# Block 1 of a fused attention and gated-FFN kernel: six plain tiles and three pairs by seven products, and token lists for the head and blocks 0 and 1

## The chip, the cores and the metric

The kernel runs on one core of a Trainium2 chip. The core has a matrix engine (PE, whose weight loads the profile lists apart as PEld), a vector engine (DVE), a scalar engine (ACT), a general engine (POOL) and a queue that issues DMAs (SP). Each works through its own list of instructions in order, and they meet through semaphores. The metric is device time in microseconds (us) of one execution.

## The reference

The first half is an attention without a score matrix, for 8 batches, 8 heads, 576 tokens and 64 channels; the second is a feed-forward block with a gated GELU on 4608 rows of 512 channels.

```python
q_s = exp(q - max(q, -1)); q_s = q_s / (sum(q_s, -1) + 1e-9)      # over the 64 channels
k_s = exp(k - max(k, 2));  k_s = k_s / (sum(k_s, 2) + 1e-9)       # over the 576 tokens
kv  = einsum('bhsd,bhse->bhde', k_s, v)
x   = einsum('bhsd,bhde->bhse', q_s, kv)      # rearranged to (4608, 512)
g   = x @ w_gate                               # (4608, 1536)
out = (0.5 * g * (1 + erf(g / sqrt(2))) * (x @ w_val)) @ w_out
```

Inputs and output are 32-bit floats; the kernel multiplies in 16-bit floats and sums in 32.

## The kernel before, in words

**Blocks.** There are nine feed-forward blocks of 512 rows, in the order 0 to 6, 8, 7. Blocks 0 to 7 take 512 of the 576 tokens of one batch each; block 8 takes the 64 left over from each. Beside a block's feed-forward the engines prepare the attention of the next batch: ACT takes the exponentials of q and k, DVE sums and inverts the norms (`norm_sum`), POOL multiplies them in (`norm_mul`), v is cast to 16 bits, PE forms kv (`unit_kv`, `unit_kv4`) and then x (`unit_x`, `unit_x4`), and copies bring x from PSUM into `xt`.

**A plain tile.** The 1536 hidden channels are 12 tiles of 128. A plain tile takes four matmuls of 512 columns for the gate (g) and four for the value (v); ACT applies Gelu to the gate's bank, DVE multiplies both into `ht`. Blocks 0 and 1 work so.

**Seven products.** In blocks 2 to 8 two tiles three apart (k and k + 3, for k in 0, 1, 2, 6, 7, 8) are one pair: a two by two block product, formed by seven products in place of eight, as in Strassen's and Winograd's scheme (`product_gv`). Each product is four matmuls of 256 columns, 28 for a pair. The price is paid elsewhere: sums of weights (`sum_wgv` for pairs 0 to 2, `sum_w1` for the others, once in the kernel), four sums of x per block (`sum_x`), copies and snapshots of PSUM banks on ACT and DVE, and sums into a buffer `cc`. The sum of weights with number 3 is written over a weight block, so that from then on those tiles can't be taken as plain ones.

**The output.** Blocks 1 to 8 use seven products there too (`product`, 12 matmuls of 256 columns each), with sums of `ht` (`sum_h`) and differences of `w_out` (`sum_w`, the tensors `tw`); block 0 uses 48 plain matmuls of 512 columns.

**Order.** Nothing is reordered by a compiler: the program's order is each engine's order. Blocks 2 to 8 are written as token lists, `PROG[b]`, that `play` reads. Tokens that matter here, for a pair k: `kP1` to `kP7` are its products (PE, banks a, b, c of the pair); `kc` copies bank a to b (ACT); `ks2`, `ks5` are snapshots; `ka2`, `ka5` sums into `cc` (DVE); `kg2`, `kg4`, `ku` Gelu (ACT); `km2`, `km4` (DVE) and `kU` write `ht`. For plain tile t: `tg`, `tv`, `tga`, `tva`. For the block: `x0` to `x3` are sums of x; `NA`, `NB`, `M0` to `M3` the next batch's norms; `K`, `X` its kv and x products, `Xa`, `Xd` the copies of x; `O1` to `O7` products of the output; `s..` sums of `ht`; `y1`, `y2`, `y5` snapshots of output banks, `b+`, `c+`, `a+` the sums into the rows to be stored, `ye` the last copy; `TE`, `TG` load ACT's tables for Exp and Gelu. A last letter d, a or p names DVE, ACT or POOL. A sign `<` in front takes the token for the block before.

**The head and blocks 0 and 1** are not lists. The head is straight code after the loads: norm sums and products of q, matmuls that only keep PE busy (`warm_pe`), transposes (`t_mm`, `t_out`), sums of exp k (`ksum_mm`), casts of v in three parts on three engines (`cast_vn`), kv (`kv_mm`, `kv_norm`) and x. Block 0's feed-forward is `ffn_first` for two tiles and `ffn_group` for the rest; its output is the loop over `mm_out`, cut at tiles 6 and 11. Block 1 calls `ffn_first`, `ffn_fi`, then `out_strassen`. What rides beside them is hung on by `at(block, kind, index, ...)` and issued by `ride`. Among it are the POOL sums of `wg` and `wv` with number 3, hung on `(1, NS, 0)`, which is after the first matmuls of block 1's output.

**PSUM** has eight banks: six in a ring (`big`), two for attention (`small`), until `one_ring` joins them.

**Buffers of sums.** One of the two `cc` buffers is a view of an `eq` tile (`cc_b`), the other a tile of its own.

Of the kernel before, what the change touches and what calls it, by code (L numbers as in the profile page):

```python
# [9 lines left out]
f32 = mybir.dt.float32  # L10
# [8 lines left out]
def kernel(  # L19
# [16 lines left out]
    P = 128  # L36
# [85 lines left out]
    for i in range(2):  # L122
# [15 lines left out]
    cc_b = [x.rearrange("p j n c -> p (j n c)").bitcast(f32)[:, 0:1024].rearrange(  # L138
        "p (i t r) -> p i t r", i=2, t=2) for x in eq_b]

# [65 lines left out]
    def cast_w_o(c, eng="pool", i0=0, i1=2):  # L206
        copy_on(eng, wo_sb[:, 2 * c + i0:2 * c + i1, :], wst[("wo", c, i0)])
# [10 lines left out]
    def cast_vn(b, j, cuts, engs):  # L218
        for n0, n1, eng in zip(cuts, cuts[1:], engs):
            copy_on(eng, v16_b[0][:, n0:n1, 2 * j:2 * j + 2, 0:D].rearrange("p n a d -> p a n d"),  # L220
                    tiles[("v", b)][:, 2 * j:2 * j + 2, n0 * D:n1 * D].rearrange("p a (n d) -> p a n d", d=D))
# [72 lines left out]
    def kv_norm(b, j, engs=("dve", "act")):  # L294
        for hh, eng in enumerate(engs):
            o, i, r = (st[(b, "kv")][:, hh, j, :], st[(b, "pskv")][hh][:, j, 0:D],
                       st[(b, "rck")][hh][:, j:j + 1])
            if eng == "act":
                nc.scalar.activation(out=o, in_=i, func=ACTF.Copy, scale=r)
            else:  # L300
                nc.vector.tensor_scalar(out=o, in0=i, scalar1=r, scalar2=None, op0=ALU.mult)

    def unit_kv(b):
        for j in range(2):
# [6 lines left out]
        for j in range(2):  # L311
            kv_norm(b, j)
# [13 lines left out]
    def kv4_norm(b):  # L326
        kv = st[(b, "kv")] = kv_tile(b)
        for hh, ps in enumerate(st[(b, "pskv4")]):
# [4 lines left out]
            if id(ps) in held:  # L333
                let_go(ps)
# [7 lines left out]
    def t_mm(b, j):  # L342
        pst = st[(b, "pst", j)] = small([P, NT - 1, P], f16, "pst") if b else big([P, NT - 1, P], f16, "pst")
        for n in range(NT - 1):
            nc.tensor.transpose(pst[:, n], buf(eq_b, b)[:, j, n + 1], ident)

    def t_out(b, j, eng):
        copy_on(eng, get_eqt(b)[:, j], st[(b, "pst", j)].rearrange("p n (h m) -> p h n m", h=2))

# [38 lines left out]
    def unit_x(b, j, spare, engs=("act", "dve")):  # L388
        px = [bank([P, MAIN], "psx", spare) for _ in range(2)]
        x_mm(b, j, px, xq)  # L390
        st[(b, "x", j)] = px
        if engs:
            x_out(b, j, engs)

    def x_out(b, j, engs=("act", "dve")):
        for t, eng in enumerate(engs):
            xt_out(b, j, t, eng, st[(b, "x", j)][t])

    def xt_out(b, j, t, eng, ps):

        copy_on(eng, get_xt(b)[:, 2 * j + t, :].rearrange("p (c m u) -> p c u m", c=(NT - 1) // 2, u=2),
                ps.rearrange("p (u c m) -> p c u m", c=(NT - 1) // 2, u=2))
# [19 lines left out]
    def x4_out(b, t, eng):  # L422
# [678 lines left out]
```

## Time and profile before

| | us |
|---|---|
| median of three runs (290.77 to 291.0) | 290.77 |
| the profiled execution | 290.9 |
| its span | 288.9 |
| head, up to block 0's first gate matmul | 14.66 |
| block 0's output starts | 36.12 |
| block 1 starts | 49.43 |
| block 1's output starts | 70.26 |
| block 2 starts | 83.85 |
| first product 5 of block 3 | 112.20 |

The span runs from the first to the last recorded instruction; about 2 us of the execution lie around it. A time in the trace is counted from the span's start. In a line of the timeline the first two numbers are the start and the length of the (merged) piece, then come engine, source line, operation, tile written, tiles read, and the number of instructions; in square brackets stands the idle time before it and what ended it. PE's pieces end later than the next one starts, since matmuls are pipelined; the distance from start to start is what one costs. In a line of waits stand the total in us, the number of times and the longest.

### The profile page before, as it was taken

The page shows a single profiled execution, that of the slowest core. Times are in us where ns is not written, and L with a number is a line of the kernel's source. Part 1 is how long each engine was busy: PE and PEld are TensorE (multiplying, and loading weights), DVE is VectorE, ACT ScalarE, POOL GpSimd, SP SyncE. Part 2 cuts the span into 40 slices and gives each one's busy share as a digit, 9 for nine tenths or more (in the row PEclk, how much of TensorE's full clock was granted, in tenths as well). Part 3 has the DMA queues.
Part 4 walks back from the last instruction along what each step waited for, and adds up shares of the span by engine and source line. Part 5 has one row for each costly group of instructions (what it writes and reads, how often), then busy time and mean ns, then how long its engine had stood idle before and what let it go on. Part 6 is the DMA issues. An engine that isn't in the chain of part 4 may idle for free.

```text
span 288.9 us, 7376 instructions
## 1 busy us (share of the span) xinstructions
PE 279.0 (97%) x2923; PEld 215.7 (75%) x2923; DVE 244.6 (85%) x491; ACT 209.5 (73%) x379; POOL 137.3 (48%) x130
## 2 busy tenths in 40 slices
PE   8799999999699999999999999999999999999994
PEld 2444444445578887888888888888888888888884
DVE  2736785587989999889999999999999899998993
ACT  3763485885388888988998899889795477716840
POOL 1867557499539640855874337541643104110110
PEclk9999999999999999999999999999999999999999
DMA  7999999958119925339139953690305030003304
GB/s 272 385 383 388 409 407 407 390 208 197 44 75 350 272 47 190 122 53 303 57 99 237 377 175 147 181 241 0 147 1 84 2 146 2 0 2 74 75 0 147
DMA packets 39122, 51.26 MB, mean 177 GB/s; under 512 B 16304, under 2 KB 22704, under 8 KB 39088
## 3 DMA queue, kind: packets, MB, share of 16 engines
q1 hardware_dynamic: 38368, 49.36, 52.2%
q10 hardware_dynamic: 720, 1.44, 1.3%
q8 instruction: 23, 0.38, 0.5%
q14 instruction: 11, 0.09, 0.1%
HBM read 37.75 MB, written 9.44 MB: 163 GB/s over the span
## 4 chain that ended last, share of the span: by engine, by line
PE 67%; DVE 4%; ACT 1%; issue 1%; DVEq 0%
PE psa L594 25%; PE psc L594 12%; PE psA L673 11%; PE psb L594 6%; PE psC L673 6%; PE psB L673 3%; PE pskv L321 1%; PE psa L673 1%; DVE sh L550 1%; PE psx L386 1%; DVE ht L800 1%; PE psc L673 0%; DVE cc L766 0%; DVE xt L193 0%; ACT L441 0%
## 5 line engine op out<-in xcount | busy, mean ns | idle before, releaser
L594 PEld LDWEIGHTS <-wgv_sb 128*128 128x128 f16 x672 | 65.7, 98 | 8.0 <-issue 0.2
L239 POOL TENSOR_TENSOR eq<-eq,rrq 128x576 f16<-128x576 f16 (+1 forms) x28 | 34.5, 1244 | 25.1 <-ACT psb L782 10.8
L673 PEld LDWEIGHTS <-ht 128*128 128x128 f16 x384 | 37.2, 98 | 5.2 <-issue 0.4
L594 PE MATMUL psa<-xs,wgv_sb 128*128 128x256 f16 x288 | 40.4, 273 | 0.0
L446 PEld LDWEIGHTS <-wgv_sb 128*128 128x128 f16 x192 | 18.6, 98 | 23.0 <-issue 1.3
L782 ACT COPY psb<-psa 128x512 f32<-128x512 f32 x42 | 24.3, 585 | 9.2 <-PE psa L594 7.2
L231 DVE TENSOR_REDUCE rq<-eq 128x18 f32<-128x1152 f16 (+1 forms) x16 | 21.2, 1324 | 5.2 <-ACT eq L213 5.0
L763 ACT ACTIVATE snq<-psc 128x512 f32<-128x512 f32 x35 | 20.7, 605 | 5.7 <-PE psc L594 5.6
L446 PE MATMUL psg<-xt,wgv_sb 128*128 128x512 f16 x96 | 23.8, 379 | 0.5 <-DVE xt L193 0.4
L446 PE MATMUL psv<-xt,wgv_sb 128*128 128x512 f16 x96 | 23.8, 379 | 0.0
L673 PEld LDWEIGHTS <-sh 128*128 128x128 f16 x192 | 18.5, 98 | 5.3 <-DVE sh L550 2.1
L213 ACT ACTIVATE ek<-kt 128x1152 f16<-128x1152 f32 (+1 forms) x11 | 17.7, 1605 | 5.6 <-issue 4.4
L594 PE MATMUL psb<-xt,wgv_sb 128*128 128x256 f16 x144 | 21.6, 273 | 0.1
L594 PE MATMUL psa<-xt,wgv_sb 128*128 128x256 f16 x144 | 20.9, 273 | 0.0
L810 POOL TENSOR_TENSOR ht<-cc 128x512 f16<-128x512 f32 x12 | 15.3, 1274 | 11.6 <-ACT cc L808 11.3
L673 PE MATMUL psA<-tw,ht 128*128 128x256 f16 x168 | 20.6, 272 | 0.0
L213 ACT ACTIVATE eq<-qt 128x1152 f16<-128x1152 f32 (+1 forms) x16 | 17.6, 1149 | 3.7 <-DMA qt<-in_q_dram 3.7
L800 DVE SCALAR_TENSOR_TENSOR ht<-psb,gl 128x256 f16<-128x256 f32 x42 | 17.3, 417 | 2.3 <-ACT gl L798 2.1
L798 ACT ACTIVATE gl<-psa 128x256 f32<-128x256 f32 x42 | 16.1, 386 | 3.2 <-PE psa L594 2.8
L798 ACT ACTIVATE gl<-psb 128x256 f32<-128x256 f32 x42 | 15.6, 383 | 3.7 <-PE psb L594 3.2
L550 POOL TENSOR_TENSOR sh<-ht 128x512 f16<-128x512 f16 x7 | 8.1, 1157 | 20.2 <-PE psc L594 11.1
L800 DVE SCALAR_TENSOR_TENSOR ht<-psa,gl 128x256 f16<-128x256 f32 x42 | 17.2, 417 | 0.2 <-ACT gl L798 0.2
(182 smaller groups left out, 692.7 us busy)
## 6 DMA issues: line engine op xcount, KB each, us to landing
qt<-in_q_dram SPq DMA_DIRECT2D x7, 1152.0 KB, 8.2
out_dram<-yo SPq DMA_DIRECT2D x15, 512.0 KB, 3.0
kt<-in_k_dram SPq DMA_DIRECT2D x6, 1152.0 KB, 8.4
vt<-in_v_dram SPq DMA_DIRECT2D x6, 1152.0 KB, 7.9
wgst<-in_moe_w_gate_dram SPq DMA_DIRECT2D x5, 512.0 KB, 7.1
wvst<-in_moe_w_val_dram SPq DMA_DIRECT2D x5, 512.0 KB, 7.1
wost<-in_moe_w_out_dram SPq DMA_DIRECT2D x5, 512.0 KB, 7.0
out_dram<-yo SPq DMA_DIRECT2D x10, 128.0 KB, 2.4
```

The costliest lines, as they stand in the source:

```text
L213: nc.scalar.activation(out=o.rearrange("p n (a d) -> p a n d", d=D), in_=tiles[(nm, b)][:, 2 * i0:2 * i1, n0 * D:NT * D].rearrange("p a (n ...
L231: nc.vector.reduce_sum(rq, e, axis=mybir.AxisListType.X)
L239: (nc.gpsimd if eng == "pool" else nc.vector).tensor_tensor(out=e, in0=e, in1=rrq.unsqueeze(-1).to_broadcast((P, n, D)), op=ALU.mult)
L446: nc.tensor.matmul(ps, w[:, ci, fi * P:(fi + 1) * P], xt[:, ci, :], start=(ci == 0), stop=(ci == HP - 1))
L550: (nc.gpsimd if eng == "pool" else nc.vector).tensor_tensor(out=o, in0=a, in1=b, op=op)
L594: nc.tensor.matmul(ps[:, t], a, x, start=(first and t == 0 and c == 0), stop=(c == 1), skip_group_check=True)
L673: nc.tensor.matmul(ps[t], a, w, start=(first and j == js[0] and (t == ts[0] or ps[t].tensor is not ps[ts[0]].tensor)), stop=(j == js[-1]), ...
L763: nc.scalar.activation(out=dst, in_=src, func=ACTF.Copy, scale=scale)
L782: nc.scalar.copy(out=t[f"b{k}"], in_=t[f"a{k}"])
L798: nc.scalar.activation(out=gl, in_=t[ps][:, 1], func=ACTF.Gelu)
L800: nc.vector.scalar_tensor_tensor(out=ht[:, k if x[2] == "2" else k + NO // 2, 0:256], in0=t[ps][:, 0], scalar=_H_SCALE, in1=t["g" + ps], o ...
L810: (nc.vector if side == "dve" else nc.gpsimd).tensor_tensor(out=ht[:, k:k + NO // 2 + 1:NO // 2, 256:512], in0=cc[:, :, 0], in1=cc[:, :, 1 ...
```

## The change

What it does:

- Block 1's tiles 6 to 11 stay plain; tiles 0 to 5 become pairs 0, 1 and 2 by seven products. The plain tiles are also started by halves: `6g:01` takes the first two of the four matmuls, `6g:23` the others.
- The head, block 0 and block 1 become lists `PROG[-1]`, `PROG[0]`, `PROG[1]`. New tokens: `@name` calls an entry of a table `extra` (its letter after a colon names the engine), `%n` issues n warming matmuls, `A`, `B`, `C` with a number are the three parts of block 0's output rows (6, 5 and 1 matmuls), `e` their copies. `ffn_first`, `ffn_group`, `ffn_fi`, `gate`, `half`, `out_strassen`, the hooks and `ride` go.
- The weight sums with number 3 of pairs 0 to 2 move to block 0: `@g3:d` on DVE and `@v3:p` on POOL. The `w_out` differences 3, 2 and 4 stand one behind the other on POOL at the end of block 0, number 1 on DVE.
- The load of block 2's v (`@lv`) becomes the last token of block 0.
- In pair 2 of block 1 `2P4` stands ahead of `2a5`.
- Both `cc` buffers are tiles of their own.
- `PROG[2]` is reordered: `y1` goes from DVE to ACT, `s24` from DVE to POOL, `x1`, `x2` for block 3 from DVE to POOL, and `x0` is put ahead of the last output products. The lists of blocks 3 to 8 hold the same tokens as before.

```diff
-    cc_b = [x.rearrange("p j n c -> p (j n c)").bitcast(f32)[:, 0:1024].rearrange(
-        "p (i t r) -> p i t r", i=2, t=2) for x in eq_b]
...
     PROG = {
-        2: ("lk lq lv 2P1 6P1 <x0d 0P1 <x2d 0P5 w71d 6P5 <x1d 6c w72d 6P2 0c w81d 6P6 0s5 0P6 6s5 0P3 6g2 w82p 6P3 "
...
-            "8u O1:25 8m2 8g4 K 7m4 8m4 O2 8U y1d TE s11d s21d s12d O5 s14d s02d s22d O6 Eq >lq b+ y5a k s24d X s04d "
-            "s13d y2a O3:03142 s23d O7 Xa Xd V2a x2d x0d O3:5 x1d"),
+        -1: ("@n0 @n1 %15 %4 @q1:p @q3:p @q2:p @s @q0:d @s0 @p0 @P0:d @r0 %3 %2 %1 @b00:d @b01:a @s1 @b10:d @b02:p "
+            "@k0 @u01:a @u00:d @z00 @Z001:d @p1 @b11:a @G0 @b12:a @P1:d @k1 @H1 @r1 @Z000:a 0g:0 1g:0 @lk0 @u11:d "
+            "1g:1 @u10:a @H0 @z01 @lk1 @lv0 @lv1 @lo @Z010:a TG 0g:1 @G1 @Z011:d"),
+        0: ("0v:0 1v:0 1v:1 0v:1 0g:23 1g:23 1ga 1v:23 @G2 1va 0v:23 @H2 @G3 @H3 @G4 0ga 0va @H4 @G5 @H5 @G6 @o0 2g "
+            "@H6 3g @o2 3ga 2v 3v 5g 5ga 3va @v1:d @o1 @g1:d 4g 4ga 2ga @v2:d 5v 7g 4v 4va 6g 6v @v3:p 5va 8v 7ga "
+            "@o3:p 6ga 6va 2va @g2:d 7v 9g 9ga 9v 9va 8g 8ga 8va 11g 10g 11ga 10ga @g4:d 10v A2 7va @E0 @g3:d @E1 "
+            "@N0 11v @N1 A0 @o5:a @lq @lk @m0:d @o4:a A3 10va @F0 @m1:p A1 B1 @T0 @F1 B0 @c0:a @m2:d @v4:d @m3:p "
+            "@c1:p 11va @t0:d @T1 @t1:d B2 @c3:p @c2:a @o5b:p @K1 C0 C1 e0d e1a C2 @z10 @Z100:a @Z101:a @z11 e2d "
+            "@Z111:d @w3:p @w1:d B3 @Z110:a @E2q @w2:p C3 @w4:p e3a TG @lv"),
+        1: ("NA 6g:01 7g:01 6v:01 7v:01 7g:23 M0 M1 7v:23 7ga 8v 10g <x0d 6g:23 6ga @tr @d1:p 6v:23 6va NB 8g 10v "
+            "10ga 8ga 9g 9ga lq 8va 7va 10va 9v 11v 0P1 lk 11g <x2d 0c 11ga <x1d 0P2 0g2 9va <x3d 0P5 1P5 0P6 0s5a "
+            "0P3 M2 0m2 11va 0s2a @sh @d0:p w61p 0a2 1P1 0P7 0a5 M3 w62p 1s5a 1P3 1c 1P6 1s2d t @d3:a 0u 1P2 1a2 2P1 "
+            "0Up 0P4 1g2 1P7 1m2 1a5 0g4 2P5 2s5d 2c 1u 2P6 2s2d 0m4 1P4 1g4 2P2 2P3 @d2:p 2P7 2P4 w64d lv 2a2 O2 "
+            "2a5 2g2 2m2 2g4 1m4 2m4 O1:03 2u 2Ud TE @E2k O1:14 s01p 1Up w63d s02p s21d O1:25 s11d O5 s12d s14d s22d "
+            "s24p y1d b+ Eq @K2 s04p O6 y5d s03p s13p V3a V2p y2d @X2 Ek O3 s23d c+ Xa @one V0a V1p TG O7 a+ O4 yea "
+            "Xd"),
+        2: ("<x0d w71d 6P1 0P1 6P5 0P5 lk <x2d 0c 0P2 6c 6s5 2P1 <x1d w72d 6P2 0P6 w81d 6P6 0s5 0P3 6g2 6P3 0s2 w82p "
...
+            "O1:4 7g4 7m4 8g4 O1:25 y1a 8m4 O2 s11d s21d O5 TE Eq >lq s12d b+ s14d K s02d s22d s04d y5a k s13d O6 "
+            "y2a s23d s24p X Xa Xd x0d x1p x2p O3:03142 O7 V2a O3:5"),
...
         if not cc_free:
-            assert b == 2
-            cc_free.extend([cc_b[0], ffn.tile([P, 2, 2, 256], f32, name="cc", tag="cc", bufs=1)])
-        if b > 2:
-            cc_free[:] = [cc_b[1] if x is cc_b[0] else x for x in cc_free]
+            cc_free.extend(ffn.tile([P, 2, 2, 256], f32, name=f"cc{i}", tag=f"cc{i}", bufs=1) for i in range(2))
...
             if len(nm) == 1:
-                mm_gv(take(x, [P, 512]), wg_sb if nm == "g" else wv_sb, xt, fi, range(HP))
+                mm_gv(t.get(x) or take(x, [P, 512]), wg_sb if nm == "g" else wv_sb, xt, fi,
+                      [int(c) for c in cis] or range(HP))
...
+        elif x[0] == "@":
+            nm, _, e = x[1:].partition(":")
+            extra[nm]({"d": "dve", "a": "act", "p": "pool"}.get(e))
+        elif x[0] == "%":
+            warm_pe(int(x[1:]))
+        elif x[0] in "ABC":
+            ns = int(x[1])
+            if x[0] == "A":
+                t[f"y{ns}"] = big([P, C], f32, "psy", True)
+            mm_out(t[f"y{ns}"], ns, {"A": range(0, NO), "B": range(NO, NFI - 1), "C": range(NFI - 1, NFI)}[x[0]])
+        elif x[0] == "e":
+            evac(b, int(x[1]), t[f"y{x[1]}"], side)
+            drop(f"y{x[1]}")
...
+    extra = {
+        "n0": on(norm_sum, 0, 0, 1), "n1": on(norm_sum, 0, 1, 1),
+        **{f"q{a}": on(norm_mul, 0, a, eng="dve") for a in range(HP)},
+        **{f"p{j}": on(t_mm, 0, j) for j in range(2)}, **{f"P{j}": on(t_out, 0, j, eng="act") for j in range(2)},
+        "s": on(kv_banks, 0), **{f"s{j}": on(ksum_mm, 0, j) for j in range(2)},
+        **{f"r{j}": on(ksum_rec, 0, j) for j in range(2)}, **{f"k{j}": on(kv_mm, 0, j) for j in range(2)},
+        **{f"b{j}{i}": on(cast_vn, 0, j, 3 * i, 3 * i + 3, eng="act") for j in range(2) for i in range(3)},
+        **{f"u{j}{h}": on(kv_norm1, 0, j, h, eng="dve") for j in range(2) for h in range(2)},
+        **{f"z{b}{j}": on(unit_x, b, j, not b or not j) for b in range(2) for j in range(2)},
+        **{f"Z{b}{j}{t}": on(xt_out, b, j, t, eng="act") for b in range(2) for j in range(2) for t in range(2)},
+        **{f"G{c}": on(cast_w, "wg", c, eng="pool") for c in range(NW)},
+        **{f"H{c}": on(cast_w, "wv", c, eng="pool") for c in range(NW)},
...
+        **{f"E{j}": on(exp, "q", 1, j, j + 1) for j in range(2)},
+        **{f"F{j}": on(exp, "k", 1, j, j + 1) for j in range(2)},
...
+        "lo": on(load_w_o, NO - 1, 1, 2), "K1": on(unit_kv, 1), **{f"w{i}": on(sum_w, i, eng="pool") for i in range(1, 5)},
+        **{f"{c}{i}": on(sum_wgv, c, i, 0, NO // 2, eng="dve") for c in "gv" for i in range(1, 5)},
+        "E2q": on(exp, "q", 2), "E2k": on(exp, "k", 2), "tr": on(unit_trem, 1), "sh": on(make_s),
+        "K2": on(unit_kv4, 2), "X2": on(unit_x4, 2, (), 1), "one": on(one_ring),
+    }
+    for b in [-1] + order:
+        for x in PROG[b].split():
+            play(max(b, 0), x)
```

## The prediction

> **What bounds the kernel now.** I read the page first, then PE's waits, then PE's timeline from 46 to 86 us (and its first 19 us), then the same stretch on DVE, ACT, POOL and the DMA queue. The page gives the span, and PE's share:
>
> ```profile
> span 288.9 us, 7376 instructions
> PE 279.0 (97%) x2923; PEld 215.7 (75%) x2923; DVE 244.6 (85%) x491; ACT 209.5 (73%) x379; POOL 137.3 (48%) x130
> ```
>
> PE is the bound nearly everywhere, so time can only come from fewer matmul columns or from the few places where PE stands still. All its waits (total, times, longest):
>
> ```profile
> PE psc L673 <- DVE sh L550: 1.8, 1, 1.8
> PE pst L345 <- POOL eq L239: 1.6, 1, 1.6
> PE pswarm L438 <- POOL ident masks.py:199: 1.4, 1, 1.4
> PE psa L673 <- DVE gl L690: 0.4, 1, 0.4
> PE psg L446 <- DVE xt L193: 0.4, 1, 0.4
> PE psc L594 <- DVE xs L582: 0.2, 1, 0.2
> ```
>
> Two lie in the head, one at the border of blocks 0 and 1, two in block 1's output, one at the end of block 2. The stages by window (block 1's plain tiles, its output with block 2's attention, block 2; each pair is busy us and instructions of PE, PEld, DVE, ACT, POOL):
>
> ```profile
> 49.43:70.26 20.83, 20.83 (x98) 9.49 (x98) 15.36 (x21) 15.24 (x23) 15.04 (x13) 1.00 0.81 264
> 70.26:83.85 13.59, 11.23 (x182) 8.95 (x180) 12.47 (x23) 8.41 (x10) 7.62 (x7) 1.00 0.30 113
> 83.85:112.20 28.35, 28.09 (x330) 24.10 (x328) 27.02 (x63) 25.13 (x49) 15.30 (x13) 1.00 0.69 213
> ```
>
> The granted clock is 1.00 in all of them. The second stretch is the poor one, and DVE's timeline says why: its sums of two SBUF tensors stretch while POOL runs its weight sums.
>
> ```profile
> 71.26 4.13 POOL L566 TENSOR_TENSOR wgv_sb<-wgv_sb 128x768 f16<-128x768 f16 x2
> ...
> 73.82 1.85 DVE L550 TENSOR_TENSOR sh<-ht 128x512 f16<-128x512 f16 x1
> 75.70 0.42 DVE L550 TENSOR_TENSOR sh<-sh,ht 128x512 f16<-128x512 f16 x1
> ```
>
> The same 512 elements take 1.85 us under POOL's sum and 0.42 us after it. PE's rates, from PE's timeline:
>
> ```profile
> 50.30 1.03 PE L446 MATMUL psv<-xt,wgv_sb 128*128 128x512 f16 x4
> 51.16 1.03 PE L446 MATMUL psg<-xt,wgv_sb 128*128 128x512 f16 x4
> ...
> 88.88 1.04 PE L594 MATMUL psa<-xs,wgv_sb 128*128 128x256 f16 x8
> 89.75 0.38 PE L594 MATMUL psc<-xs,wsv 128*128 128x256 f16 x2
> ```
>
> Start to start: 0.86/4 = 0.216 us for 512 columns, 0.87/8 = 0.109 us for 256.
>
> **Part 1, fewer columns.** Six plain tiles leave (48 matmuls of 512: 48 x 0.216 = 10.37 us), three pairs come (3 x 28 of 256: 84 x 0.109 = 9.17 us): -1.2 us. Weight loads rise from 48 to 84; one lasts 98 ns, under the 109 ns of a matmul, and block 2 runs densely with that mix, so they stay hidden. Here a page speaks against the change: the Trainium skill, "TensorE: Matmul & The Clock Gate", section "Back-to-back issue gap", gives about 131 ns for a matmul of 512 columns and 81 ns for 128 in a sustained stream; with some 98 ns between them for 256 (my estimate), part 1 would be 8.2 - 6.3 = +1.9 us. The rows above contradict it.
>
> **Part 2, the head.** In the old order the first transpose (8.88) waits for POOL's product of q1, 7.35 to 8.83. In the new list both sums of block 0 stand ahead of `@q0:d` on DVE: the second reciprocal ends at 9.55, q0 takes 0.69, so the transpose starts near 10.3, 1.4 late. The four warming matmuls and `@s0` now run before it. Its copy moves from ACT, where it ended at 11.96 behind exp k, to DVE: 10.95 + 0.69, near 11.7. But POOL now does q3 (to 11.15), q2 (1.0 to 1.5) and only then the cast `@b02:p` (0.54): 12.7 to 13.2, and `@k0` waits for it, against 12.37 before. From there the old steps (0.57 to the scaling, 1.04 to the x product) and the new order of copies end the first two tiles at 19.1 to 19.5 instead of 18.86: +0.25 to +0.6, taken +0.4. Lower bound -0.1 (q2 in 1.0 and the copies free at once), upper +0.8. Weights do not bind: tile 2's gate chunk is cast by 16.87, PE takes it at 18.86.
>
> **Part 3, the border of blocks 0 and 1.** The last output matmul starts at 48.68 and lasts 0.22, block 1 starts at 49.43: 0.53 us idle, the wait for xt among them. The list puts both x products ahead of `B3` and `C3`, six matmuls (1.3 us) that cover the copies: -0.5. If it fails, 0. The price is on ACT: from near 47.9 it runs e1a, Z100, Z101, Z110, E2q, e3a, TG, by start-to-start distances in the rows 0.48 + 3 x 0.58 + 2.26 + 0.48 + 1.40, so `7ga` starts at 54.3 and ends at 54.9. PE, from 49.85, asks for its bank after 24 matmuls and two transposes, at 55.2. Margin 0.3: 0, at worst +0.6.
>
> **Part 4, block 1's middle.** DVE has 18 to 20 us of work in a stage of 19.7 on PE: two norm sums 3.2, six `va` 4.0, six `m` 2.4, six `a` 4.1, three `s` 2.0, four x sums and `w64d` 2.1, remains of block 0 1.7. It fits, with 1.4 us in hand before `0a2`. POOL now has `w3`, `w2`, `w4` in a row, 3.10 each by the old tw rows: 46.1 to 57.1 with the wait for `@w1:d` near 50.9. `<x0d`, a sum of two SBUF tensors, reaches DVE's head at 54.1, as `w4` starts; behind it stand `6va` (its bank is 9g's), NB, 8va, 7va, 10va. If it goes first: 0.42. If POOL goes first: up to 3.1, 9g waits about 1.2, and x2d, x1d, x3d can each meet an M product or a w sum of 1.16. Bounds 0 and +3.3; taken +0.7, near a lost race for x0d with half recovered, since in blocks 2 to 8 such sums took 0.42 in the median beside a busy POOL. The Trainium skill, "SBUF — State Buffer", section "Who interferes with whom", says that the port pair is an exclusive lock, and that the later of a two-input DVE operation and a reading GpSimd one waits for the whole of the earlier; the 1.85 us row agrees. By it alone x0d would wait the full 3.1, and the part would be nearer +1.2. The list issues `2P4` ahead of `2a5` (which then reads bank a with product 4 in it), so PE waits for nothing between them. The second bank copy, `2c`, may cost 0.1 and is in the 0.7.
>
> **Part 5, block 1's output.** Before: 13.59 us for 84 x 0.109 + pskv 0.77 + x products 0.85 = 10.8 us of PE, so 2.8 idle. After, counted from 2P4's end: O2 and O1 need 2.6, and `O5` waits at j = 1 for 2u, 2Ud, w63d, s21d, s11d: 0.55. `@K2` waits for ACT: 2u, table load and preload 1.40, exp k 2.12, so K2 stands 0.7. `O7 a+ O4` are adjacent: O4 must wait until DVE has read bank A: 0.17 drain + 0.05 + 0.69 = 0.9 (before, block 2's x products stood between). Together 2.1 against 2.8: -0.7. The other side: none of them -2.8, all late by another microsecond +1. The Exp of k's first half and its table load leave block 1's plain part; ACT has room there, so nothing is gained by that.
>
> **Part 6, block 2.** The stretch of 28.35 us holds 240 matmuls x 0.109 + 0.77 + 0.85 = 27.8 us of PE work; the 0.5 left is idle time just ahead of block 3's 0P5, at 112.2, which waits for x0. The new list puts `x0d` ahead of O3 and O7, gives x1, x2 and `s24` to POOL, and y1 to ACT, about 1.9 us less on DVE: -0.5, other side 0.
>
> **At nothing.** `@lv` now stands behind the store that waits for e3a: v of block 2 is issued near 53.5, not 45.49. Its first reader on POOL comes after M1, near 59.5; K2 needs it at 75. Without that cover POOL's M2 slips by what v is late. In the DMA queue the store, lv, lq, lk and the transposes (64, needed at 77) keep order with several us in hand. The own cc tiles change no order; `v3:p` and `g3:d` fall in block 0, where DVE is idle a third of the time.
>
> **Sum.** +0.4 - 0.5 - 1.2 + 0.7 - 0.7 - 0.5 = -1.8 us. The profiled execution took 290.9 (span 288.9 and 2.0 around it), 0.13 over the median of the runs, 290.77: 289.1 for it, 289.0 for the median.
>
> **Rivals.**
> (a) *The lock takes the gain; slower.* One mechanism: DVE's two-input sums in block 1 queue behind POOL's three tw sums and its M and w sums. Full price +3.3 in part 4 instead of 0.7: +0.8, 291.6. It decides from 2.5 us of delay on, which is what the other parts give. For it: the 1.85 us row, and 9.3 us of tw sums in a row. Against it: blocks 2 to 8 hold as much POOL work and show PE without gaps.
> (b) *The output only swaps its waits; no change.* ACT reaches E2k a microsecond later, and K2 and O4 wait as long as the old sums: part 5 at +0.5, total -0.6, 290.2. For it: the chain 2P4, 2a5, 2u, table load, exp is serial, and each delay reaches PE in full. Against: POOL is free of the 4.13 us of sums that stretched DVE.
> (c) *Block 1 runs as densely as block 3.* No waits in part 4 and half of those in part 5: -0.7 - 1.0 more, about 287.3. Against it: O4 behind a+.
>
> **How the numbers follow.** Forecast 0.53 (its own range 288.2 to 290.1), (a) 0.2, (b) 0.17, (c) 0.1. About 0.2%, 0.58 us, is what a measurement of this kernel can tell from no change, so slower by that means over 291.35, faster under 290.19. Forecast, (c) and a little of (b) make faster 0.64; the rest of (b) and the mild end of (a) same 0.17; (a) slower 0.19. The range reaches from (c) to (a): 287.0 to 291.7.
>
> **What would show it.** Part 1: 84 matmuls L594 in block 1, 0.109 apart. Part 2: tile 2's first gate matmul at 19.1 to 19.5. Part 3: no PE wait for xt near 49.8. Part 4: the first xs sum of DVE near 54, its length 0.4 or 3; PE's wait ahead of 9g. Part 5: PE waits for ek at K2 and for DVE's yo at O4, each under 1 us. Part 6: no PE wait for xs at the start of block 3. Wrong if POOL's tw sums end well after 57 or the head loses over 1 us.

## The result

The changed kernel took 288.9 us (median of 20 executions, 288.34 to 291.7) against 290.93 for the kernel before (20, 290.75 to 292.39): a ratio of 0.9935, 95% interval 0.9912 to 0.9957. It is faster by 2.0 us; 289.0 was predicted.

In 9 of 32 executions of the changed kernel (the 20 above and 12 of the repetition below) and in 23 of 54 of the old one, timed beside the experiments, the mean granted TensorE clock of the whole execution is 0.985 to 0.994 in place of 0.997 to 1.0, and these lie above the others: those of before by 1.4 us, seven of the nine of the changed kernel by 2.4 to 3.1 us, the other two by 1.2 and 1.5. For the 20 executions of before above no clock is on record; eight of them lie where those with the lowered clock do (292.1 to 292.39). "At full clock" below means the median without them: 290.9 before, 288.64 changed.

The execution profiled first was one with a lowered clock (291.06 us, clock 0.986, span 289.2). Its windows over the head say where (length, then busy us and instructions of PE, PEld, DVE, ACT, POOL, then the granted clock):

```profile
7.20:9.57 2.37, 0.00 (x1) 0.00 (x2) 1.56 (x3) 1.90 (x2) 1.05 (x1) 1.00 1.04 406
9.57:12.00 2.43, 2.28 (x49) 1.38 (x50) 1.64 (x5) 1.57 (x2) 2.38 (x3) 0.87 1.05 373
12.00:14.00 2.00, 1.75 (x74) 1.04 (x72) 0.94 (x3) 0.17 (x1) 1.12 (x2) 0.50 1.08 377
14.00:16.00 2.00, 1.88 (x32) 1.25 (x36) 0.97 (x3) 1.59 (x4) 0.92 (x2) 0.50 1.09 387
16.00:18.00 2.00, 2.00 (x39) 0.70 (x31) 1.02 (x4) 0.31 (x1) 1.80 (x3) 0.50 1.08 374
```

PE stands until 9.57, and from about 12 to 18 us it gets half the clock; from there on the clock is whole. Tile 2's gate starts at 21.10; before, it started at 18.86. To read the change itself I use a repetition, the same kernel profiled at clock 1.0 (288.67 us, span 286.8). Its windows over block 0 from tile 2's gate, block 1's tiles, block 1's output, and block 2 up to block 3's first product 5:

```profile
18.91:49.04 30.13, 30.07 (x225) 14.17 (x224) 20.68 (x35) 17.35 (x27) 21.76 (x19) 1.00 1.06 401
49.04:69.05 20.01, 19.93 (x136) 12.90 (x135) 18.40 (x27) 14.83 (x27) 18.73 (x15) 1.00 0.82 272
69.05:82.15 13.10, 11.17 (x182) 8.90 (x180) 12.14 (x27) 12.14 (x15) 7.80 (x8) 1.00 0.46 142
82.15:109.89 27.74, 27.74 (x330) 24.19 (x328) 26.00 (x60) 24.45 (x50) 17.57 (x15) 1.00 0.65 201
```

Against before (these stages start at 18.86, 49.43, 70.26, 83.85, and the last ends at 112.20) that is 30.57 to 30.13, 20.83 to 20.01, 13.59 to 13.10 and 28.35 to 27.74. Block 2 is now without a gap (27.74 busy of 27.74). The output is still the poor stretch, with 11.17 busy of 13.10. Its PE timeline, with the idle time and its releaser in brackets:

```profile
71.67 0.60 PE L624 MATMUL psC<-tw,sh 128*128 128x256 f16 x4
72.66 1.05 PE L624 MATMUL psC<-tw,sh 128*128 128x256 f16 x8 [0.40 <-DVE sh L496]
74.46 0.78 PE L318 MATMUL pskv<-v,ek 64*64 64x65 f16 x72 [0.75 <-ACT ek L210]
...
80.84 1.47 PE L624 MATMUL psA<-tw,ht 128*128 128x256 f16 x12 [0.78 <-DVE yo L663]
```

These are the three waits that the prediction named: `O5` for the sums of `ht` (0.40), `@K2` for exp k (0.75), `O4` behind `a+` (0.78). The old 1.8 us wait for a sum of `ht` is gone; three new ones hold 1.9.

### The profile page after: what moved, and what is told of

It reads as the page before. It is cut to its first block, busy times and chain, and to the rows that moved or that the text cites. A ratio compares the mean times of both kernels' runs of the same rounds, so it can differ in the third digit from the quotient of the medians.

```text
span 289.2 us, 7456 instructions
## 1 busy us (share of the span) xinstructions
PE 278.9 (96%) x2959; PEld 220.0 (76%) x2959; DVE 247.8 (86%) x499; ACT 212.2 (73%) x392; POOL 146.0 (50%) x136
## 3 DMA queue, kind: packets, MB, share of 16 engines
q10 hardware_dynamic: 720, 1.44, 1.3%
## 4 chain that ended last, share of the span: by engine, by line
PE 89%; DVE 4%; ACT 3%; DMA 2%; issue 0%; SPq 0%
PE psa L540 27%; PE psA L624 14%; PE psc L540 13%; PE psC L624 7%; PE psb L540 7%; PE psB L624 3%; DMA qt<-in_q_dram 2%; PE psx L383 2%; PE pskv L318 2%; DVE rq L227 1%; ACT eq L210 1%; DVE eq L235 1%; PE psy L449 1%; ACT ek L210 1%; PE pswarm L433 1%; PE ps10g L441 1%
## 5 line engine op out<-in xcount | busy, mean ns | idle before, releaser
L540 PE MATMUL psa<-xs,wgv_sb 128*128 128x256 f16 x312 | 43.4, 273 | 0.0
L707 POOL TENSOR_TENSOR ht<-cc 128x512 f16<-128x512 f32 x20 | 26.0, 1303 | 31.4 <-ACT cc L705 29.3
L705 ACT ACTIVATE cc<-cc 128x512 f32<-128x512 f32 x45 | 28.3, 630 | 9.1 <-DVE cc L663 9.1
L679 ACT COPY psb<-psa 128x512 f32<-128x512 f32 x45 | 26.1, 586 | 9.7 <-PE psa L540 7.5
L663 DVE SCALAR_TENSOR_TENSOR cc<-psa,snq 128x512 f32<-128x512 f32 x45 | 30.6, 685 | 2.5 <-PE psa L540 1.7
L663 DVE SCALAR_TENSOR_TENSOR cc<-psc,snq 128x512 f32<-128x512 f32 x45 | 30.3, 685 | 2.4 <-PE psc L540 1.4
L624 PE MATMUL psA<-tw,ht 128*128 128x256 f16 x192 | 23.5, 272 | 0.8 <-DVE yo L663 0.8
L540 PE MATMUL psb<-xt,wgv_sb 128*128 128x256 f16 x156 | 23.4, 273 | 0.0
L540 PE MATMUL psa<-xt,wgv_sb 128*128 128x256 f16 x156 | 22.9, 273 | 0.0
L697 DVE SCALAR_TENSOR_TENSOR ht<-psb,gl 128x256 f16<-128x256 f32 x45 | 18.7, 416 | 2.0 <-ACT gl L695 1.8
```

The source lines that it names most:

```text
L540: nc.tensor.matmul(ps[:, t], a, x, start=(first and t == 0 and c == 0), stop=(c == 1), skip_group_check=True)
L624: nc.tensor.matmul(ps[t], a, w, start=(first and j == js[0] and (t == ts[0] or ps[t].tensor is not ps[ts[0]].tensor)), stop=(j == js[-1]), ...
L663: nc.vector.scalar_tensor_tensor(out=out, in0=src, scalar=scale, in1=sn, op0=ALU.mult, op1=ALU.add)
L679: nc.scalar.copy(out=t[f"b{k}"], in_=t[f"a{k}"])
L697: nc.vector.scalar_tensor_tensor(out=ht[:, k if x[2] == "2" else k + NO // 2, 0:256], in0=t[ps][:, 0], scalar=_H_SCALE, in1=t["g" + ps], o ...
L705: nc.scalar.activation(out=cc[:, :, 1], in_=cc[:, :, 1], func=ACTF.Gelu, scale=1.0 / _H_SCALE)
```

## The experiments

All were timed beside the kernel before; kernels timed together share its executions. Between two executions of the same instructions the start of block 1 differs by up to 0.9 us (48.8 to 49.7 in the profiles below, where POOL's casts of weights come a little sooner or later), so beside the median stands a second measure from the profile: the time from block 1's first matmul to block 3's first product 5. It is read from one execution each. In r0, e2 and e6, which have the same lists of blocks 1 and 2, it agrees within 0.07 us; in e1, which has them too, it is 0.6 longer.

| kernel | median, us (range, n) | ratio to before, 95% interval | at full clock | block 1 to block 3 |
|---|---|---|---|---|
| before | 290.95 (290.77-292.52, 17) | | 290.91 | 62.77 |
| changed, again (r0_after) | 289.05 (288.38-291.28, 12) | 0.9935, 0.9909-0.9961 | 288.64 | 60.85 |
| ten more warming matmuls (e1_warm) | 289.48 (289.15-290.07, 6) | 0.9937, 0.9913-0.9962 | 289.48 | 61.48 |
| old order of q (e2_qorder) | 288.70 (288.60-289.51, 6) | 0.9913, 0.9889-0.9938 | 288.70 | 60.90 |
| before, POOL's sums moved alone (e3_poolsums) | 289.20 (289.04-290.55, 6) | 0.9932, 0.9905-0.9959 | 289.17 | 60.96 |
| e2 with 2a5 ahead of 2P4 (e4_a5first) | 289.39 (288.98-290.48, 7) | 0.9937, 0.9913-0.9961 | 289.39 | 61.21 |
| e2 with O4 later (e5_o4late) | 289.17 (288.79-290.56, 6) | 0.9932, 0.9906-0.9958 | 289.11 | 61.17 |
| e2 with v loaded earlier (e6_lvearly) | 288.95 (288.65-290.28, 6) | 0.9926, 0.9901-0.9951 | 288.88 | 60.83 |
| e2 without pairs in block 1 (e7_twelve) | 288.09 (287.56-289.46, 6) | 0.9893, 0.9867-0.9919 | 287.96 | 60.28 |
| e2, ends of the pairs reordered (e8_chain) | 289.92 (289.49-290.59, 9) | 0.9954, 0.9937-0.9972 | 289.92 | 61.89 |
| e7 with a new end of the output (e9_tail) | 287.35 (286.98-288.95, 6) | 0.9876, 0.9846-0.9905 | 287.30 | 59.85 |
| e2 with O6 ahead of K2 (e10_o6first) | 288.49 (288.26-288.98, 5) | 0.9886, 0.9861-0.9911 | 288.49 | 60.62 |
| e10 with e9's end (e11_o6tail) | 288.79 (288.17-290.03, 6) | 0.9900, 0.9871-0.9930 | 288.66 | 60.75 |

Beside e10 and e11 eight of eleven executions of before had the lowered clock, so their ratios flatter them; at full clock before took 290.88 there.

**What the head does, and what the moved sums are worth.** The changed kernel once more:

> The changed kernel once more, for its profile and spread. Theory H (clock): in the profiled execution PE stood idle from 7.2 to 9.57 us and was granted 0.50 of its clock from about 11.6 to 18 us; executions without that drop should end near 288.4 to 288.9, those with it near 291. In an execution without the drop tile 2's first gate matmul should start at 18.5 to 19.1 (21.10 with it). Rival D: the spread comes from the loads, then the head is late by DMA waits at a granted clock of 1.00.

The ratio came again, with three lowered clocks in twelve executions.

The head with ten more warming matmuls ahead of the first transposes:

```diff
-        -1: ("@n0 @n1 %15 %4 @q1:p ...
+        -1: ("@n0 @n1 %15 %14 @q1:p ...
```

> Ten more warming matmuls ahead of the sums of exp k in the head, so that PE is busy from 1.4 to about 9.4 us. Theory H: the clock stays at 1.00 in every execution, median 288.4 to 288.6, none above 289.5. Rival D: same spread as the changed kernel, median 288.9, some near 291.

No lowered clock in six executions, and tile 2's gate at 18.86. The median did not fall, though: all six lie at 289.15 or above, where 288.4 to 288.6 was expected. In the profiled execution something else came between. POOL stood for the DMA of block 2's v, its chain in block 1 was late by more than a microsecond, and one of its sums then lay under DVE's `2Ud`. POOL's and DVE's timelines:

```profile
60.65 0.67 POOL L186 CAST v<-vt 128x576 f16<-128x576 f32 x1 [2.04 <-DMA vt<-in_v_dram]
...
70.72 1.15 POOL L496 TENSOR_TENSOR sh<-sh,ht 128x512 f16<-128x512 f16 x1
```

```profile
70.75 1.67 DVE L707 TENSOR_TENSOR ht<-cc 128x512 f16<-128x512 f32 x1
```

The same `2Ud` takes 0.69 where POOL is still; here it took 1.67, and PE's wait at `O5` grew from 0.4 to 1.4. Whether that holds for the other five is not shown.

The old order of q, inside the new list:

```diff
-        -1: ("@n0 @n1 %15 %4 @q1:p @q3:p @q2:p @s @q0:d @s0 @p0 ...
+        -1: ("@n0 @q0:d @q1:p @n1 @q2:d @q3:p %15 @p0 %4 @s @s0 ...
```

> The old order of q's sums and products, with the first transposes ahead of the four warming matmuls, in the changed kernel's head. My step for the head (+0.4 us at full clock): the transposes start at 8.9 instead of 10.2, tile 2's gate at 18.5 to 18.9, and the gap on PE shrinks from 2.4 to 1.6 us, so under theory H the clock drops less often: median 288.0 to 288.5. Rival: the q order is hidden behind the cast of v and exp k, tile 2's gate does not move, median as the changed kernel's.

The first transpose starts at 8.80, tile 2's gate at 18.66, both as expected, and the median misses the 288.0 to 288.5: at full clock it is that of the changed kernel (288.70 and 288.64). In the eight later profiles with this head tile 2's gate lies between 18.67 and 19.19, so its 0.25 us against r0's 18.91 is not clear of the scatter, and the order of q is worth nothing that these runs show. The lowered clock is rarer: in the nine kernels with this head (e2, e4 to e11) 5 of 57 executions had one, and they lay 1.4 to 1.7 us high. That it is the order of q which makes it rarer is not shown, since the kernel before has that order too, and 23 of 54.

The kernel before, with nothing but POOL's sums moved: those of `wg` and `wv` with number 3 from after the first output matmuls into block 1's plain tiles, three of `sum_w1` to the end of block 0.

```diff
-    at(0, NS, 8, L(x_out, 1, 1), L(sum_w, 1), L(sum_w, 2, "pool"), L(exp, "q", 2), L(preload, ACTF.Gelu))
+    at(0, NS, 8, L(x_out, 1, 1), L(sum_w, 1), L(sum_w, 2, "pool"), *(L(sum_w1, x, NO, "pool") for x in (1, 2, 4)),
+       L(exp, "q", 2), L(preload, ACTF.Gelu))
...
-    at(1, NS, 0, L(sum_wgv, "g", 3, 0, NO // 2, "pool"), L(sum_wgv, "v", 3, 0, NO // 2, "pool"))
-    for i, x in ((6, 1), (6, 2), (6, 4), (9, 3)):
+    at(1, FI, 6, L(sum_wgv, "g", 3, 0, NO // 2, "pool"), L(sum_wgv, "v", 3, 0, NO // 2, "pool"))
+    for i, x in ((9, 3),):
```

> The kernel before with one thing changed: its POOL weight sums are moved out of block 1's output (g3 and v3 to tile 6, three sums of pair 6 to the end of block 0). Theory L (DVE's two-input sums wait for POOL's): DVE's sums take 0.42 to 0.92 us in place of 1.0 to 1.85, PE's wait of 1.8 us ahead of product 5 goes, and the time falls by 1.5 to 2.3 us, to 288.5 to 289.3. Rival: the sums are late for their own data, the wait stays, 290.5 to 291.

This edit alone takes 1.8 us out from block 1 to block 3 (62.77 to 60.96), where the whole change takes 1.9; at full clock the medians fall by 1.7 and 2.3. On POOL the sums end by 70.6, and the output's sums of `ht` on DVE behind that take 0.41 and 0.68. POOL first, then DVE:

```profile
65.81 3.23 POOL L566 TENSOR_TENSOR wgv_sb<-wgv_sb 128x768 f16<-128x768 f16 x2
69.01 1.60 POOL L575 TENSOR_TENSOR wgv_sb<-wgv_sb 128x512 f16<-128x512 f16 x1
```

```profile
71.68 0.68 DVE L550 TENSOR_TENSOR ht<-ht 128x1024 f16<-128x1024 f16 x1
...
73.48 0.41 DVE L550 TENSOR_TENSOR sh<-ht 128x512 f16<-128x512 f16 x1
```

The output shrinks from 13.59 to 11.79 us, 1.3 us below the changed kernel's. So the changed kernel does not lack this gain; it gives most of it back. To what, the twelve plain tiles below (e7) show.

**Four edits of the list, each by itself, on the kernel with the old order of q.** `2a5` ahead of `2P4`, as in every other pair:

```diff
-            "... 2P7 2P4 w64d lv 2a2 O2 2a5 2g2 ..."
+            "... 2P7 2a5 2P4 w64d lv 2a2 O2 2g2 ..."
```

> The kernel with the old order of q in the head (288.7 us, output of block 1 from 68.83 to 81.98) with one change: in pair 2 of block 1, 2a5 goes back ahead of 2P4, so PE waits until DVE has read bank a before product 4 writes it. Theory (part 4 counts the swap as a gain of PE's wait): PE stands for DVE's sum at 2P4, 0.4 to 0.9 us, and as O2 and the Gelu 2u come later by as much, K2 does too: 289.2 to 289.6. Rival: 2a5 comes that much earlier on DVE, so 2u, 2Ud, s21, s11 and exp k come earlier and the waits at O5 (0.4) and K2 (0.75) shrink by what 2P4 waits: 288.7 within 0.2.

PE's waits in this stretch:

```profile
PE psa L540 <- DVE cc L663: 0.8, 1, 0.8
PE psA L624 <- DVE yo L663: 0.8, 1, 0.8
PE pskv L318 <- ACT ek L210: 0.6, 1, 0.6
```

`2P4` waits 0.8, but `O5` no longer waits and `K2` 0.15 less: block 1 to block 3 grows by 0.3. The swap is worth 0.3 us. Both theories were half right; the median, 0.7 up, also holds a block 1 that started 0.9 late in the profile.

`O4` and its copy behind the first eight matmuls (two products) of block 2, with `Xd` ahead of `O3`:

```diff
-            "... @X2 Ek O3 s23d c+ Xa @one V0a V1p TG O7 a+ O4 yea Xd"),
-        2: ("<x0d w71d 6P1 0P1 6P5 0P5 ...
+            "... @X2 Ek s23d Xd O3 c+ Xa @one V0a V1p TG O7 a+"),
+        2: ("<x0d w71d 6P1 0P1 <O4 <yea 6P5 0P5 ...
```

> The kernel with the old order of q in the head (288.7 us) with one change at the end of block 1: Xd stands ahead of O3, and O4 with its copy stands in block 2 behind the first products of pairs 6 and 0, so that they lie between O7 and O4. Theory (O4 waits 0.78 us for DVE's a+): the wait goes, the stretch from block 1's output to the end of O4 is 0.6 to 0.8 shorter: 288.0. Rival: the wait goes elsewhere, to s23 for O7, to x0 for product 5 in block 2, or to the first product behind Xd, 288.5 to 288.9.

The rival: the wait moved on. PE's timeline shows 0.29 left at `O4`, and 0.30 at product 2 of pair 0, whose bank copy `0c` now stands behind the copy `yea` on ACT. By the distances from start to start the two places cost 0.62 and 0.46 us beyond their matmuls, 1.08 together, where `O4` cost 0.95 in e2. So nothing was gained, and the median, 289.17, lies even above the rival's 288.5 to 288.9.

```profile
81.59 1.47 PE L623 MATMUL psA<-tw,ht 128*128 128x256 f16 x12 [0.29 <-DVE yo L662]
...
84.23 0.60 PE L540 MATMUL psb<-xt,wgv_sb 128*128 128x256 f16 x4 [0.30 <-ACT psb L678]
```

The load of v ahead of block 0's stores:

```diff
-            "... @o5b:p @K1 C0 C1 e0d e1a C2 ... @w4:p e3a TG @lv"),
+            "... @o5b:p @K1 C0 C1 @lv e0d e1a C2 ... @w4:p e3a TG"),
```

> The kernel with the old order of q in the head (288.7 us, executions from 288.6 to 289.5) with one change: the load of block 2's v stands ahead of block 0's first store in SP's queue, not behind its last one. Theory (in some executions v comes late, POOL's chain in block 1 slips and its sums meet DVE's 2Ud and s21): no wait of POOL for v, its first cast of v at 58.5 or earlier, PE's wait at O5 at most 0.4 in the profile, all executions within 0.3 us of 288.5. Rival (v is in time and the spread is from the order in which DVE and POOL reach the shared port): the same spread of 0.9 us and the same median.

POOL no longer waits for v (0.63 in e2), and neither the median nor the spread at full clock (288.65 to 289.46, before 288.60 to 289.51) changes. That is the rival. The late v of e1's profiled execution is real, but loading v earlier does not take the spread away. What makes it is not settled.

Block 1 with twelve plain tiles; the sums with number 3 on DVE behind tile 5:

```diff
-            "... 9v 11v 0P1 lk 11g <x2d 0c 11ga <x1d 0P2 0g2 9va <x3d 0P5 1P5 0P6 0s5a ... 2P7 2P4 w64d lv 2a2 O2 ..."
+            "... 9v 11v lk 11g 11ga 9va 3g 3ga M2 3v 11va 3va @sh @d0:p w61p 4g 4ga 4v 4va M3 w62p 5g 5ga 5v t 5va
+            @d3:a @v3:d @g3:d 0g 0ga 0v 0va 1g 1ga @d2:p 1v 1va 2g 2ga 2v w64d lv 2va O2 ..."
```

> The kernel with the old order of q in the head (288.7 us) with block 1's pairs undone: its tiles 0 to 5 are plain again, 48 matmuls of 512 columns for 84 of 256; the two weight sums with number 3 stand on DVE behind tile 5, the sums of x for block 1 go. Theory (part 1: -1.2 of columns, less 0.4 of waits that the pairs bring): the stretch from block 1's first matmul to its output 20.8 us in place of 20.0, time 289.3 to 289.7. Rival (pairs give nothing, since what they put on DVE, ACT and POOL delays the output by as much): the middle is longer by 0.8 but the output, with DVE free of a and s, is shorter by 0.4 or more: 288.7 to 289.1.

Beyond both: this kernel, with the new lists and without the pairs, is the faster one, by 0.6 to 0.7 us. Its windows over tiles, output and block 2, and its `K2` on PE:

```profile
48.72:69.55 20.83, 20.83 (x99) 9.50 (x98) 13.37 (x20) 12.31 (x21) 17.38 (x14) 1.00 0.82 266
69.55:81.26 11.71, 10.93 (x181) 8.98 (x180) 10.35 (x23) 11.68 (x14) 5.99 (x7) 1.00 0.44 147
81.26:109.00 27.74, 27.74 (x330) 24.19 (x328) 25.99 (x60) 24.07 (x49) 17.60 (x15) 1.00 0.68 201
```

```profile
73.57 0.78 PE L318 MATMUL pskv<-v,ek 64*64 64x65 f16 x72
```

| us | before | e3: sums alone | e7: lists, no pairs | e2: lists and pairs |
|---|---|---|---|---|
| block 1's tiles | 20.83 | 20.82 | 20.83 | 20.01 |
| block 1's output | 13.59 | 11.79 | 11.71 | 13.15 |
| block 2 | 28.35 | 28.35 | 27.74 | 27.74 |

The table takes the change apart. The pairs bring 0.82 in the tiles and cost 1.44 in the output. The moved sums bring 1.8 there. The new lists bring 0.6 in block 2; which of the moves in `PROG[2]` does it no run tells. ACT's timeline shows how the pairs reach the output; first the changed kernel, whose output starts at 69.05, then e7, at 69.55:

```profile
69.97 0.38 ACT L695 ACTIVATE gl<-psa 128x256 f32<-128x256 f32 x1 [1.59 <-DVE cc L663]
70.25 0.62 ACT L705 ACTIVATE cc<-cc 128x512 f32<-128x512 f32 x1
70.89 1.28 ACT L436 ACT_TABLE_LOAD   x1
72.19 0.20 ACT L436 ACTIVATE tiny<-tiny 128x1 f32<-128x1 f32 x1
72.30 2.11 ACT L210 ACTIVATE ek<-kt 128x2304 f16<-128x2304 f32 x1
```

```profile
68.89 0.60 ACT L718 ACTIVATE gl<-ps2g 128x512 f32<-128x512 f32 x1 [1.13 <-PE ps2g L441]
69.50 1.28 ACT L436 ACT_TABLE_LOAD   x1
```

A plain tile ends with its gate's Gelu, done before the value's matmuls end. A pair ends with products, then two sums on DVE, then two Gelus on ACT; only then can the table for Exp come. It starts 1.84 us after the output does, in e7 0.05 us before; the exponential of k follows it, `K2` follows that, 5.41 us after the output's start in place of 4.02.

**Can the pairs be kept without that price, and how far does e7 go?** Pairs 1 and 2 with their products 3 and 7 first, others between `2P7` and `2P4`:

```diff
-            "... 0u 1P2 1a2 2P1 0Up 0P4 1g2 1P7 1m2 1a5 0g4 2P5 2s5d 2c 1u 2P6 2s2d 0m4 1P4 1g4 2P2 2P3 @d2:p 2P7 2P4 ..."
+            "... 0u 1a2 2P1 0Up 0P4 2c 2P5 1P7 0g4 2s5d 1a5 2P6 1P2 2s2d 0m4 1g2 2P3 1P4 1u 1g4 @d2:p 1m2 2P7 lv 2a2
+            2P2 2a5 O2:03 1m4 2P4 2g2 2u 2m2 O2:1425 ..."
```

> The kernel with the old order of q in the head (288.7 us; middle 20.01, output 13.15 with waits of 0.45 at O5 and 0.75 at K2) with the pairs of block 1 kept, but the end of pairs 1 and 2 reordered: products 3 and 7 first, then 1P4, 2P2 and a third of O2 between 2P7 and 2P4, with 2a5 ahead of 2P4 again; the copy of s11 ahead of s21. The same instructions, other order. Theory (the pairs' price in the output is the chain 2P7, 2a5, 2u, table load, exp k, and 2u, 2Ud, s21, s11, which stands uncovered behind the last pair): the waits at O5 and K2 go, output 12.0, middle 20.0 to 20.3, time 287.4 to 287.9. Rival (the chain is not the cause, DVE and POOL have too much work there anyway): the output stays above 12.7, or the middle grows by what the output loses: 288.5 to 289.0.

A miss, by 2 us. PE's timeline says why:

```profile
65.50 0.39 PE L540 MATMUL psc<-xs,wsv 128*128 128x256 f16 x2 [0.71 <-DVE cc L663]
...
69.94 0.60 PE L540 MATMUL psa<-xs,wgv_sb 128*128 128x256 f16 x4 [0.34 <-DVE cc L663]
...
74.60 0.78 PE L318 MATMUL pskv<-v,ek 64*64 64x65 f16 x72 [0.57 <-ACT ek L210]
```

`2P5`, pulled forward, needs the PSUM bank that `1a2` gives back, and waits 0.71 for it; everything behind slips, and `2u` ran at 69.98 where it had run at 70.09 in e2. The chain was hardly shortened, so this run does not say whether it is the cause. `O5` no longer waits, and `K2` still does, until exp k is done: as long as `K2` waits behind it, `O5`'s wait costs nothing by itself.

e7 with `O4` behind twelve matmuls (three products) of block 2 and its copy behind `0c` and `6c`, `x0` ahead of `a+`:

```diff
-            "... @X2 Ek O3 s23d c+ Xa @one V0a V1p TG O7 a+ O4 yea Xd"),
-        2: ("<x0d w71d 6P1 0P1 6P5 0P5 lk <x2d 0c 0P2 6c 6s5 ...
+            "... @X2 Ek s23d Xd O3 c+ Xa @one V0a V1p TG O7"),
+        2: ("<x0d <a+ w71d 6P1 0P1 6P5 <O4 0P5 lk <x2d 0c 0P2 6c <yea 6s5 ...
```

> The kernel with twelve plain tiles in block 1 and the old order of q (288.1 us; its one wait in the output is 0.78 at O4, behind a+) with the end of the output changed: Xd ahead of O3, x0 ahead of a+, O4 behind twelve products of block 2, its copy behind the copies 0c and 6c. Theory: the wait at O4 goes and, unlike where O4 stood behind eight products and its copy ahead of 6c, no other takes its place: 287.3 to 287.6. Rival: it moves on again, to product 5 or to the copies of the bank: 287.9 to 288.3.

As the theory had it, and the fastest of all: 287.35, with block 1 to block 3 shorter by 0.43. The 0.78 at `O4` is gone; 0.19 at product 5 of pair 6 takes its place:

```profile
80.22 0.61 PE L540 MATMUL psc<-xs,tw 128*128 128x256 f16 x4 [0.19 <-DVE xs L528]
```

**The pairs' wait covered from the other side.** Products as in e2; `O6` ahead of `K2`, so that exp k has 1.31 us more, `O3` ahead of the x products:

```diff
-            "... 2u 2Ud TE @E2k O1:14 s01p 1Up w63d s02p s21d O1:25 s11d O5 s12d s14d s22d s24p y1d b+ Eq @K2 s04p O6 y5d
-            s03p s13p V3a V2p y2d @X2 Ek O3 s23d c+ ..."
+            "... 2u s01p 1Up s02p s11d 2Ud TE @E2k O1:14 s21d O1:25 O5 s04d y1d s12d s22d s24p s03p s13p O6 s14d y5d b+
+            Eq @K2 w63d V3a V2p O3:142503 y2d w64d @X2 Ek s23d c+ ..."
```

> The kernel with the pairs and the old order of q in the head (288.7 us; output of block 1 13.15 us with waits of 0.45 at O5, 0.75 at K2 and 0.78 at O4), its products as they are, but the output reordered: O6 ahead of K2, O3 ahead of X2, s11 ahead of 2Ud, s04 on DVE, w64 late. Theory (what the pairs cost in the output is that exp k, ready 5.4 us after the output starts, holds K2; O5's wait lies in K2's shadow): O6's 1.31 us of matmuls cover it, K2 waits 0.1 or less, output 12.0 to 12.5, time 287.6 to 288.1. Rival (DVE's and POOL's sums of ht bind as closely as exp k does): O6 waits for y1 or s12, or O3 for s24 and y5, by 0.7 or more together, 288.5 to 289.2.

```profile
73.92 1.47 PE L624 MATMUL psA<-tw,sh 128*128 128x256 f16 x12 [0.18 <-DVE gl L658]
75.33 0.78 PE L318 MATMUL pskv<-v,ek 64*64 64x65 f16 x72
...
79.54 0.61 PE L624 MATMUL psA<-tw,ht 128*128 128x256 f16 x4 [0.36 <-DVE ht L496]
```

`O5` and `K2` wait no more, as the theory said. The output is 12.58 us, 0.57 shorter, just past the theory's 12.5; 0.18 and 0.36 of new waits for DVE stand in it, and block 2 gives 0.3 back (28.04). In all 0.28 from block 1 to block 3, and 288.49, the rival's edge (288.5) and not the theory's 287.6 to 288.1. That exp k held `K2` is shown; that it is the whole price of the pairs is not, since DVE's sums bind next.

The same with e9's end:

> The same reordered output, and the end of block 1 as in the kernel with twelve plain tiles and O4 behind twelve products of block 2, which took 287.35 us (0.74 less than without that end). Theory: 0.7 below the other kernel of this call, 286.9 to 287.4, so that with the pairs as with plain tiles the waits can be put away. Rival (the gain of that end needs DVE as free as twelve plain tiles leave it): at most 0.3 below the other kernel.

The rival: nothing gained (60.75 after 60.62). The wait at `O4` goes, and the first product of block 2 waits 0.55 for `Xa`, which stands on ACT behind the next exp k; that ran at 77.38 here and at 75.57 in e9, 1.1 us later when counted from block 1's start.

## Why the prediction was right, and where it was not

The time was right to 0.1 us at the median, and that closeness is luck: at full clock the change brings 2.3 where 1.8 was forecast, and the executions with a lowered clock put 0.26 back on the median of the twenty. By its steps, measured between the two profiles at full clock:

| step | predicted | measured |
|---|---|---|
| part 2, head up to tile 2's gate | +0.4 | +0.05 |
| part 3, border | -0.5 | -0.44 |
| parts 1 and 4, block 1's tiles | -1.2 + 0.7 | -0.82 |
| part 5, output | -0.7 | -0.49 |
| part 6, block 2 | -0.5 | -0.61 |
| sum | -1.8 | -2.31 |

The sum reaches to block 3's first product 5; the whole span is 2.1 shorter (288.9 to 286.8), so 0.2 is lost again behind it. By stage no step is off by more than 0.4. Parts 2 and 3 rest on one profile each, and the scatter of the start of block 1 is larger than they are. In eight of eleven profiles with the new lists of head and block 0 the stretch from tile 2's gate to block 1 takes 30.02 to 30.27 us, in the other three 30.41 to 30.81, against 30.57 before.

*Part 2.* The first transpose came at 10.35, as worked out, and the head lost almost nothing by it at full clock: `@k0`, which the step let wait for POOL's cast of v until 12.7 to 13.2, started at 12.48, and the cast, done at 12.68, did not hold it. What the step also lacked is the clock, which is lowered in 9 of 32 executions of the changed kernel; the profiled one lost 2.2 us to it in the head. The prediction took the granted clock of one profile, 1.00 throughout, for the clock of every execution.

*Part 3* held: the last output matmul of block 0 now runs into block 1 without a gap, and PE's wait for xt is gone.

*Part 1* held in its columns. The 216 and 109 ns give 20.8 for twelve tiles, as e7 has it (20.83), and 19.6 for the mix, against which 20.01 was seen. The rule of the Trainium skill that the prediction weighed against it ("TensorE: Matmul & The Clock Gate", "Back-to-back issue gap") would, by the prediction's estimate from it, have made the stretch longer by 1.9 us; it got 0.82 shorter.

*Part 4* was mis-sized: 0.4 for 0.7. `x0d` came at 52.19, 1.9 us sooner than worked out, so it met `w2`, the first of POOL's two sums, and did not wait for the second, `w4`. DVE and POOL at full clock:

```profile
52.19 1.65 DVE L528 TENSOR_TENSOR xs<-xt 128x512 f16<-128x512 f16 x1
54.65 0.69 DVE L722 SCALAR_TENSOR_TENSOR ht<-ps6v,gl 128x512 f16<-128x512 f32 x1 [0.81 <-ACT gl L719]
```

```profile
50.47 6.33 POOL L477 TENSOR_TENSOR tw<-wo_sb,tw 128x1536 f16<-128x1536 f16 x2 [0.90 <-DVE tw L477]
```

Of the merged row the first sum runs from 50.47 to 53.56; `x0d`, alone worth 0.42, ended at 53.84, 0.28 behind it. That agrees with the Trainium skill, "SBUF — State Buffer", section "Who interferes with whom", by which the later of the two waits for the whole of the earlier. It cost no PE wait, because DVE then stood 0.8 us for ACT's Gelu anyway. Rival (a) fell with that. Most of what the part did cost, 0.24 of 0.38, is the second bank copy, `2c`, for which the prediction had 0.1: `2P6` writes the bank that `2c` copies, and starts 0.46 behind the two matmuls before it in place of 0.22, as the copy ends (66.37). PE and ACT:

```profile
65.97 0.38 PE L540 MATMUL psc<-xs,wsg 128*128 128x256 f16 x2
66.43 0.38 PE L540 MATMUL psa<-xs,wsv 128*128 128x256 f16 x2
```

```profile
65.78 0.59 ACT L679 COPY psb<-psa 128x512 f32<-128x512 f32 x1
```

*Part 5* named its three waits and their sizes well (0.55, 0.7 and 0.9 against 0.40, 0.75 and 0.78). Its failure lies elsewhere: it booked these waits as what the output has left, and did not ask whose they are. Two of the three belong to part 1. e7, without the pairs, has neither, and e3 shows that the moved sums alone bring 1.8 in this stretch. Part 1 was costed by what it does to PE in its own stage; its last pair's chain, in the next stage, costs more than the columns bring. So the forecast's total was right, and its account of which part earns it was wrong: the pairs of the title, as these lists place them, cost 0.6 us, where parts 1 and 4 gave them a gain of 0.5. Rival (b), that the output only swaps its waits, described what the pairs did: 1.4 of the 1.8 that the sums had freed.

One choice of the new lists lies in between. The kernel before took the first half of exp k in block 1's plain part, and only the second half behind the last Gelu, 1.16 us long:

```profile
71.51 1.16 ACT L213 ACTIVATE ek<-kt 128x1152 f16<-128x1152 f32 x1
```

The changed kernel takes all of it there, 2.11 us; the prediction put this at nothing. No run puts the first half back beside the pairs, so how much of `K2`'s 0.75 this choice costs stays open.

*Part 6* held: the wait for xs ahead of block 3 is gone, and block 2 is 0.61 shorter.

*At nothing:* `@lv` at nothing is borne out by e6's median, though in e1's profiled execution v came late and `O5` waited a microsecond longer for it. That PE waits for nothing around `2P4` is true and worth 0.3, not the 0.8 that the wait itself shows when it is put back.

## What to carry to other kernels

A part that saves work in one stage is to be costed up to the point where the next stage's first long chain ends: ask what the last unit of the stage leaves behind it. A change of several parts is to be taken apart on the chip even when its total is as forecast, since here one part earned most of it (1.7 of 2.3 at full clock) and the part in the title lost; keeping the lists and leaving the pairs out, with a new end of the output, gave 287.35. And a PE wait that stands ahead of another one is worth only what both lose together.

## What the hardware showed that I had not expected

The granted clock can fall to 0.50 for some 6 us in the head: one trace shows it. By the mean clock of each execution, it falls in some executions and not in others with the same instructions: 9 of 32 of the changed kernel, 23 of 54 of before, 5 of 57 of the lists with the old order of q. In the one trace that shows it, the drop follows 2.4 us without a recorded matmul. The Trainium skill, "TensorE: Matmul & The Clock Gate", Part 1, gives half clock after an idle window of about 3.4 us that runs freely; the trace's 0.50 agrees, and its gap is shorter, though some matmul records may be missing in it. The length of the gap alone does not decide: in e4, e5 and e8 PE stood 2.8 us ahead of the first transposes, and the granted clock stayed at 1.00. PE in e8:

```profile
8.93 0.62 PE L341 MATMUL pst<-ident,eq 128*128 128x128 f16 x8 [2.81 <-POOL eq L235]
```

So the cause of the drop is open: ten more warming matmuls gave none in 6 executions, which a rate of 9 in 32 gives by chance in about one case of seven, and no lowered execution of before was traced.
